# Attention and two feed-forward layers on one core: seven plain chunks and one Strassen unit of 1024 tokens in place of six and two of 768, weight sums on VectorE, later attention steps, more buffers

## The chip, the core and the metric

The kernel runs on one core of one Trainium2 chip. The metric is the device time of one execution in microseconds (us). Times of a kernel are medians over several executions; the profile is one further execution, taken with the hardware profiler. TensorE (PE) multiplies, VectorE (DVE), ScalarE (ACT) and GpSimd (POOL) work elementwise, and SyncE (SP) issues almost all DMAs from one queue. Each engine takes its own instructions in the order in which the program lists them.

## The reference

Three layers follow each other: linear attention with an RMS norm over 8 batches of 576 tokens (4608 tokens of 512 features), a bilinear feed-forward layer without a nonlinearity behind it, and a feed-forward layer with SiLU.

```python
kv = np.einsum('bhsd,bhse->bhde', k, v)
out = np.einsum('bhsd,bhde->bhse', q, kv)
rms = np.sqrt(np.mean(out * out, axis=-1, keepdims=True) + 1e-06)
x = out / rms * g_norm            # then transposed to (4608, 512)
a = x @ w1; b = x @ w2            # 512 -> 1024 each
x2 = ((a * b) @ w3) @ w_out       # 1024 -> 1024 -> 512; the kernel multiplies w3 @ w_out first
h = x2 @ w_in                     # 512 -> 2048
result = (h * (1.0 / (1.0 + np.exp(-h)))) @ w_out2   # 2048 -> 512
```

## The kernel before, in words

Every big product is made of three matmuls: both operands are split into a high part (rounded to fp32r by ScalarE) and a low part (the rest, by VectorE), and high x high, high x low and low x high are added in PSUM (`passes`, lines 111 to 115, and `run`, line 786). A split is therefore one ScalarE cast and one VectorE subtraction.

The tokens are cut into 9 chunks of 512. The program has three stretches.

**Start.** w3 @ w_out is formed (tiles `wps`, then `wch`, `wcl`), and the attention of chunk 0 is done.

**Plain phase.** The chunks in `PLAIN` (six of nine) go through the bilinear layer directly. A chunk has 8 steps; a step j has 12 matmuls into `pa` (x @ w1), 12 into `pb` (x @ w2), the product `asb` = pa * pb (ScalarE copies pa, VectorE multiplies, line 738), its split into `ch` and `cl`, and 12 matmuls of the step before into four banks `x2ps` (line 555, `g2_mm`). All these matmuls stream 512 columns. After the last step of a chunk ScalarE and VectorE copy two `x2ps` banks each into `x2o` tiles, and SP stores these to DRAM as `x2d` (lines 562 to 574).
Between the groups of 12 matmuls, other work is put by a table of events (lines 583 to 616): `event(gap, ...)` with three gaps to a step. The attention of chunk c starts at its own gap: `kv_load` and `kv_mm` (k, v and their product), `q_load`, `att_a` (matmuls `o`), `att_b` (squares `sq` and copies `ob`, ScalarE), `att_c` (matmuls `s`, the sums of squares), `att_d` (three ScalarE operations), `att_e` (two VectorE operations on `u`, then its split into `rh` and `rl`), `att_r` (matmuls `rb`, which spread `rh` and `rl` over the features), `att_x` (VectorE multiplies `ob` by `rb`) and `att_f` (the split into `xh`, `xl` for a plain chunk; a store to DRAM as `xd` for a chunk in `LATER`). Two PSUM banks, `att`, serve all these matmuls.
Also in this phase the weights of the later products are prepared, piece by piece. `ensure(done - 1)` calls `advance` (line 293) once: it stores what is ready (`flush`), loads piece n+3 (`raw`), casts piece n-1 (`bh`, line 275), decodes piece n+1 on ScalarE (lines 169, 170) and piece n on VectorE (lines 201, 203), and subtracts for piece n-1 (line 280). Three pieces make a block of weights; for every second piece of a triple, 28 times in all, `block_sums` (lines 236 to 249) forms the four sums that Strassen's scheme needs, on GpSimd, of 256 columns each, into `s12` and `s34`. `advance` is called two or three times in a step. Results go to DRAM as `wbd`.

**Strassen phase.** `UNITS` lists units of work; a unit of width w covers 2w tokens and does products of 2 x 2 blocks with 7 instead of 8 block products (Winograd's form). Units "A" do the bilinear layer for the chunks in `LATER` (6 blocks of 7 runs of 12 matmuls, each of w columns), units "B" the SiLU layer for all tokens (8 such blocks). The loop at line 919 runs over the blocks; the last block of a unit follows the first block of the next one. All matmuls are at line 799 (tiles `ps`); operands are split at lines 701 and 702, and the operand sums are on GpSimd (line 689).

## Time and profile before

| | us |
|---|---|
| median of 3 executions (1500.31 to 1504.01) | 1500.82 |
| the profiled execution | 1503.21 |
| its span, first to last instruction | 1501.1 |
| of it the start, until the first `pa` | 87.3 |
| plain phase, until the first `ps` | 530.1 |
| units A and the first B block among them | 198.2 |
| the rest of the B units | 685 |

PE is busy for 95% of the span by its records, DVE for 61%, ACT for 45%, POOL for 29%; the DMA engines moved 229 GB/s on average. A busy time of PE is not PE at its peak, since matmuls overlap in the records: how far apart they start says more. "Granted clock" (PEclk) is the share of the full TensorE clock, 1.0 for 2.4 GHz and 0.5 for 1.2 GHz. In a view of waits, "X <- Y" means that X was idle and that Y ended the wait.

### The profile page before, as it was taken

Reading aid. Unit: us, or ns where it says so; the run is one execution under the profiler, and the core shown is the slowest. Engines: PE = TensorE matmul, PEld = TensorE weight load, DVE = VectorE, ACT = ScalarE, POOL = GpSimd, SP = SyncE. Lnnn points to the kernel's source line nnn. Section 1 sums busy time; section 2 is a strip of 40 time slices with the busy share of each in tenths; the row PEclk is TensorE's granted clock in tenths of the full one; section 3 lists DMA queues with packets and bytes.
Section 4 is the critical chain, followed back from the end, with each engine's and each line's share of the span. In section 5 each row is a group of like instructions: output and inputs, shape, how many; then the busy total and the mean of one; then the engine's idle time right before and its main releaser. Section 6 shows DMA issues by size and latency. Waiting matters only on the chain.

```text
span 1501.1 us, 20241 instructions
## 1 busy us (share of the span) xinstructions
PE 1420.7 (95%) x7328; PEld 1193.1 (79%) x7328; DVE 918.0 (61%) x1208; ACT 677.6 (45%) x1099; POOL 428.8 (29%) x269
## 2 busy tenths in 40 slices
PE   7889898998897989999999999999999999999998
PEld 4567675676676657999998878787878888999998
DVE  7757555464545543448476568756785667468558
ACT  7765534344443632325153434453544443545443
POOL 0000122122221211034343354335353425245222
PEclk9999999999898999999999999999999999999999
DMA  9654467768676845488977766776668667987876
GB/s 327 206 168 163 160 229 245 262 208 274 197 243 195 270 165 183 138 297 256 348 239 252 237 186 195 229 261 191 190 206 272 190 195 245 314 246 247 291 246 206
DMA packets 160258, 344.22 MB, mean 229 GB/s; under 512 B 15264, under 2 KB 79776, under 8 KB 160160
## 3 DMA queue, kind: packets, MB, share of 16 engines
q1 hardware_dynamic: 159584, 341.90, 70.5%
q8 instruction: 58, 0.95, 0.3%
q10 hardware_dynamic: 576, 1.05, 0.2%
q14 instruction: 40, 0.33, 0.1%
HBM read 269.48 MB, written 73.40 MB: 228 GB/s over the span
## 4 chain that ended last, share of the span: by engine, by line
PE 76%; DMA 9%; DVE 6%; ACT 3%; issue 2%; SPq 2%; POOL 2%; POOLq 0%; DVEq 0%; ACTq 0%
PE ps L799 57%; DMA wbd<-s 3%; PE pb L113 2%; PE pb L115 2%; PE pb L114 2%; PE x2ps L113 2%; DMA raw<-wb_l 1%; PE pa L113 1%; PE x2ps L114 1%; PE x2ps L115 1%; PE pa L114 1%; PE pa L115 1%; DMA raw<-w3t_l 1%; PE rb L419 1%; DMA v<-v_l 1%
## 5 line engine op out<-in xcount | busy, mean ns | idle before, releaser
L799 PE MATMUL ps<-xo,w 128*128 128x384 f32 (+1 forms) x2352 | 466.8, 358 | 0.2
L799 PEld LDWEIGHTS ps<-xo,w 128*128 128x128 f32 x2352 | 422.2, 188 | 41.4 <-ACT u L831 1.7
L799 PE MATMUL ps<-go,w 128*128 128x384 f32 (+1 forms) x2016 | 414.1, 364 | 6.4 <-issue 6.4
L799 PEld LDWEIGHTS ps<-go,w 128*128 128x128 f32 x2016 | 364.3, 189 | 52.7 <-issue 12.9
L702 DVE TENSOR_TENSOR go<-g,go 128x768 fp32r<-128x768 f32 (+1 forms) x120 | 163.3, 1365 | 120.7 <-ACT go L701 120.2
L809 DVE TENSOR_TENSOR c<-ps,c 128x512 f32<-128x512 f32 (+1 forms) x280 | 162.2, 616 | 27.2 <-PE ps L799 26.2
L689 POOL TENSOR_TENSOR g_t<-g 128x768 f32<-128x768 f32 (+1 forms) x48 | 119.1, 2482 | 131.0 <-DVE g L881 65.6
L689 POOL TENSOR_TENSOR g<-g,g_t 128x768 f32<-128x768 f32 (+1 forms) x24 | 50.9, 2123 | 355.4 <-DVE go L702 355.4
L245 POOL TENSOR_TENSOR s<-t 128x256 f32<-128x256 f32 x28 | 23.2, 829 | 421.9 <-DMA wbd<-s 210.7
L701 ACT CAST go<-g 128x768 fp32r<-128x768 f32 (+1 forms) x120 | 110.9, 945 | 48.1 <-PE ps L799 40.1
L702 DVE TENSOR_TENSOR go<-g_t,go 128x768 fp32r<-128x768 f32 (+1 forms) x48 | 96.5, 2010 | 21.0 <-ACT go L701 21.0
L831 ACT COPY s<-ps 128x512 f32<-128x512 f32 (+1 forms) x40 | 21.7, 543 | 154.7 <-PE ps L799 154.7
L738 DVE TENSOR_TENSOR asb<-pb,asb 128x512 f32<-128x512 f32 x48 | 33.0, 688 | 92.6 <-PE pb L115 79.7
L113 PE MATMUL pb<-xh,w2h 128*128 128x512 f32 x192 | 83.3, 434 | 0.9 <-DVE asb L738 0.5
L113 PE MATMUL x2ps<-ch,wch 128*128 128x512 f32 x192 | 78.0, 406 | 5.6 <-ACT x2o L573 3.4
L115 PE MATMUL pb<-xh,w2l 128*128 128x512 f32 x192 | 78.8, 410 | 1.4 <-DVE w2l L230 1.4
L114 PE MATMUL pb<-xl,w2h 128*128 128x512 f32 x192 | 79.1, 412 | 0.0
L113 PE MATMUL pa<-xh,w1h 128*128 128x512 f32 x192 | 76.3, 398 | 0.0
L114 PE MATMUL pa<-xl,w1h 128*128 128x512 f32 x192 | 75.8, 395 | 0.0
L115 PE MATMUL pa<-xh,w1l 128*128 128x512 f32 x192 | 75.5, 393 | 0.0
L114 PE MATMUL x2ps<-cl,wch 128*128 128x512 f32 x192 | 75.5, 393 | 0.0
L115 PE MATMUL x2ps<-ch,wcl 128*128 128x512 f32 x192 | 75.3, 392 | 0.0
(113 smaller groups left out, 1919.5 us busy)
## 6 DMA issues: line engine op xcount, KB each, us to landing
w<-wbd SPq DMA_DIRECT2D x364, 512.0 KB, 4.4
wbd<-bh SPq DMA_DIRECT2D x72, 256.0 KB, 3.7
raw<-wb_l SPq DMA_DIRECT2D x32, 512.0 KB, 5.4
wbd<-s SPq DMA_DIRECT2D x56, 256.0 KB, 3.7
q<-q_l SPq DMA_DIRECT2D x36, 256.0 KB, 3.9
raw<-w3t_l SPq DMA_DIRECT2D x16, 512.0 KB, 6.0
k<-k_l SPq DMA_DIRECT2D x32, 256.0 KB, 4.2
v<-v_l SPq DMA_DIRECT2D x32, 256.0 KB, 4.5
```

The lines of the kernel that those rows point to most:

```text
L113: nc.tensor.matmul(out=ps_out, lhsT=ah, rhs=bh, start=first, stop=False)
L114: nc.tensor.matmul(out=ps_out, lhsT=ah, rhs=bl, start=False, stop=False)
L115: nc.tensor.matmul(out=ps_out, lhsT=al, rhs=bh, start=False, stop=last)
L245: nc.gpsimd.tensor_tensor(out=s1, in0=a21, in1=a22, op=ALU.add)
L419: nc.tensor.matmul(out=o, lhsT=spread[rows, :], rhs=half_[rows, :], start=n == 0, stop=n == 1, skip_group_check=True)
L689: nc.gpsimd.tensor_tensor(out=x, in0=x if a == place else self.src[a], in1=x if b == place else self.src[b], op=ALU.subtract)
L701: nc.scalar.copy(out=t[:, 0, :, :self.w], in_=x)
L702: self.cuts[n].tensor_tensor(out=t[:, 1, :, :self.w], in0=x, in1=t[:, 0, :, :self.w].bitcast(F32), op=ALU.subtract)
L738: nc.vector.tensor_mul(out=asb, in0=pb, in1=asb)
L799: mm = lambda a, bb, start, stop: nc.tensor.matmul(out=o, lhsT=a, rhs=bb, start=start, stop=stop, skip_group_check=True)
L809: eng.tensor_tensor(out=out_, in0=a, in1=b, op=ALU.add)
L831: nc.scalar.copy(out=t[nm, d], in_=o)
```

## The change

- `PLAIN` gets a seventh chunk, so `LATER` has two chunks (4 and 8) and one unit A of width 512 (1024 tokens) does them; before, two units A of width 384 did three chunks. The B units stay.
- `block_sums` runs on VectorE; `s12` gets two buffers, and the `bh` tiles (tag `wh`) four in place of three.
- `q` and `x2o` tiles have four buffers in place of two; all four `q_load` of a chunk are issued together, 9 gaps before that chunk's attention begins (2 before that of chunk 8).
- The attention of a chunk takes 20 gaps in place of 18, and `att_r`, `att_x` and `att_f` come two gaps later behind `att_e` (17 and 18 in place of 15 and 16).
- `advance` is called twice in a step, not two or three times; there are 8 more steps.
- `dynamic_dma_scratch_size=1024` frees SBUF, from which the buffers come.

```diff
-PLAIN = (0, 1, 2, 4, 5, 6)
+PLAIN = (0, 1, 2, 3, 5, 6, 7)
-UNITS = (("A", 384), ("A", 384), ("B", 512), ("B", 512), ("B", 512), ("B", 384), ("B", 384))
+UNITS = (("A", 512), ("B", 512), ("B", 512), ("B", 512), ("B", 384), ("B", 384))
...
-        s12 = cv.tile([P, N], F32, tag="s12", bufs=1, name=f"s12_{n}")
+        s12 = cv.tile([P, N], F32, tag="s12", bufs=2, name=f"s12_{n}")
...
-        nc.gpsimd.tensor_tensor(out=s1, in0=a21, in1=a22, op=ALU.add)
+        nc.vector.tensor_tensor(out=s1, in0=a21, in1=a22, op=ALU.add)
...
-            h = cv.tile([P, N], F32R, tag="wh", bufs=3, name=f"bh{n}_{op}")
+            h = cv.tile([P, N], F32R, tag="wh", bufs=4, name=f"bh{n}_{op}")
...
-        t = at.tile([P, N], F32, tag="q", bufs=2, name=f"q{c}_{p}")
+        t = at.tile([P, N], F32, tag="q", bufs=4, name=f"q{c}_{p}")
...
-                    o = at.tile([P, N], F32, tag="x2o", bufs=2, name=f"x2o{c}_{m}")
+                    o = at.tile([P, N], F32, tag="x2o", bufs=4, name=f"x2o{c}_{m}")
...
-            for p in range(2):
-                event(max(gap, gap_was + 11), q_load, c, p)
+            for p in range(KD):
+                event(gap_was + 11, q_load, c, p)
...
-            event(gap + 15 + i, att_r, c, i)
-            event(gap + 15 + i, att_x, c, i)
-            event(gap + 15.5 + i + 1.5 * (c in LATER), att_f, c, i)
+            event(gap + 17 + i, att_r, c, i)
+            event(gap + 17 + i, att_x, c, i)
+            event(gap + 17.5 + i + 1.5 * (c in LATER), att_f, c, i)
...
-        gap += 18 if c + 1 < B else 11
+        gap += 20 if c + 1 < B else 13
...
-                for _ in range(2 - j % 2):
-                    ensure(done - 1)
+                ensure(done - 1)
...
-    nc = bacc.Bacc("TRN2", target_bir_lowering=False, num_devices=1)
+    nc = bacc.Bacc("TRN2", target_bir_lowering=False, num_devices=1, dynamic_dma_scratch_size=1024)
```

The other three sums change engine like the first; two of the four `q_load` were in the loop over `att_a` at gap + 7 before.

What this moves is seen in the order of the instructions. On PE, at the attention of chunk 2, which falls into the first steps of chunk 1: before, the first `rb` matmuls stand between `pa` and `pb` of step 1, and since the matmuls `s` there are three groups of 12 (`pb` of step 0, `x2ps`, `pa` of step 1).

```order
L115 MATMUL pa1_1_1754<-xh1_1229,w1l1_163 128x512
L419 MATMUL rb2_0_1767<-rh2_1750,spread_113 128x512
L419 MATMUL rb2_1_1768<-rh2_1750,spread_113 128x512
L419 MATMUL rb2_0_1767<-rl2_1751,spread_113 128x512
L419 MATMUL rb2_1_1768<-rl2_1751,spread_113 128x512
L113 MATMUL pb1_1_1792<-xh1_1229,w2h1_164 128x512
```

Now they stand behind `pb` of step 2, and five groups of 12 lie between `s` and `rb` (`pa` and `pb` of step 1, `x2ps`, `pa` and `pb` of step 2).

```order
L115 MATMUL pb1_2_1850<-xh1_1291,w2l2_931 128x512
L419 MATMUL rb2_0_1866<-rh2_1788,spread_112 128x512
L419 MATMUL rb2_1_1867<-rh2_1788,spread_112 128x512
L419 MATMUL rb2_0_1866<-rl2_1789,spread_112 128x512
L419 MATMUL rb2_1_1867<-rl2_1789,spread_112 128x512
L113 MATMUL x2ps1_0_1803<-ch1_1_1783,wch1_133 128x512
```

At all other chunks, too, three groups became five. On DVE, at the same place, from the multiplication `asb` of step 0 to the low part `rl` and its use: before, the last `x2o` copies stand straight ahead of the two operations on `u`.

```order
L738 TENSOR_TENSOR asb1_0_1676<-pb1_0_1678,asb1_0_1676 128x512
L109 TENSOR_TENSOR cl1_0_1692<-asb1_0_1676,ch1_0_1691 128x512
L181 TENSOR_TENSOR t44_1707<-w1h0_158,w1l0_159 128x512
L280 TENSOR_TENSOR s34_41_1586<-s34_41_1586,bh43_5_1705 128x512
L571 COPY x2o0_1_1739<-x2ps0_1_1102 128x512
L571 COPY x2o0_3_1745<-x2ps0_3_1104 128x512
L405 SCALAR_TENSOR_TENSOR u2_1695<-s2_1660,u2_1695 128x512
L406 SCALAR_TENSOR_TENSOR u2_1695<-u2_1695,r2_1694 128x512
L109 TENSOR_TENSOR rl2_1751<-u2_1695,rh2_1750 128x512
L426 TENSOR_TENSOR ob2_0_1536<-rb2_0_1767,ob2_0_1536 128x512
```

Now `asb` of step 1 stands between the copies (line 571) and `u`, and `rl` is followed by the low part `cl` of step 1, with the use of `rb` further down.

```order
L280 TENSOR_TENSOR s34_41_1585<-s34_41_1585,bh43_5_1702 128x512
L571 COPY x2o0_1_1730<-x2ps0_1_1101 128x512
L571 COPY x2o0_3_1736<-x2ps0_3_1103 128x512
L735 TENSOR_TENSOR asb1_1_1768<-pb1_1_1770,asb1_1_1768 128x512
L405 SCALAR_TENSOR_TENSOR u2_1758<-s2_1739,u2_1758 128x512
L406 SCALAR_TENSOR_TENSOR u2_1758<-u2_1758,r2_1757 128x512
L109 TENSOR_TENSOR rl2_1789<-u2_1758,rh2_1788 128x512
L109 TENSOR_TENSOR cl1_1_1784<-asb1_1_1768,ch1_1_1783 128x512
```

The sums of a block of weights were on POOL (here those of pieces 46 and 47):

```order
L245 TENSOR_TENSOR s12_47_1830<-t46_1720 128x256
L246 TENSOR_TENSOR s12_47_1830<-s12_47_1830,t47_1777 128x256
L247 TENSOR_TENSOR s34_47_1831<-t47_1777,t46_1720 128x256
L248 TENSOR_TENSOR s34_47_1831<-t47_1777,s12_47_1830 128x256
```

On DVE they now stand between the decoding of the second piece and the subtractions for the piece before, ahead of the next `asb`:

```order
L201 SCALAR_TENSOR_TENSOR z47_1797<-raw47_1700,z47_1797 128x512
L203 SCALAR_TENSOR_TENSOR t47_1796<-t47_1796,z47_1797 128x512
L245 TENSOR_TENSOR s12_47_1840<-t46_1764 128x256
L246 TENSOR_TENSOR s12_47_1840<-s12_47_1840,t47_1796 128x256
L247 TENSOR_TENSOR s34_47_1841<-t47_1796,t46_1764 128x256
L248 TENSOR_TENSOR s34_47_1841<-t47_1796,s12_47_1840 128x256
L280 TENSOR_TENSOR t46_1764<-t46_1764,bh46_0_1834 128x256
L280 TENSOR_TENSOR s34_44_1709<-s34_44_1709,bh46_5_1836 128x512
L735 TENSOR_TENSOR asb1_2_1848<-pb1_2_1850,asb1_2_1848 128x512
```

## Rows read from the trace of the kernel before

**Rows 1.** The page: busy time of PE, and granted clock in 40 slices.
```profile
PE 1420.7 (95%) x7328; PEld 1193.1 (79%) x7328; DVE 918.0 (61%) x1208; ACT 677.6 (45%) x1099; POOL 428.8 (29%) x269
...
PEclk9999999999898999999999999999999999999999
```

**Rows 2.** Windows, all engines: length, busy of PE, PEld, DVE, ACT, POOL; PEclk, DMA.
```profile
87.30:617.40 530.10, 480.48 (x2578) 361.08 (x2577) 272.17 (x426) 233.66 (x423) 103.81 (x116) 0.95 0.63 206
617.40:815.60 198.20, 196.19 (x1093) 191.88 (x1092) 120.41 (x168) 77.75 (x131) 68.29 (x31) 0.99 0.83 269
815.60:1240.90 425.30, 422.43 (x1849) 345.83 (x1849) 283.00 (x285) 189.70 (x252) 163.28 (x60) 1.00 0.70 218
576.50:617.30 40.80, 40.80 (x181) 33.81 (x181) 13.38 (x16) 9.55 (x14) 7.37 (x4) 1.00 0.44 154
```

**Rows 3.** Timeline of PE, Strassen phase: start, length, operation, count; 384 columns, then 512.
```profile
617.37 58.43 PE L799 MATMUL ps<-xo,w 128*128 128x384 f32 x336
675.64 14.72 PE L799 MATMUL ps<-go,w 128*128 128x384 f32 x84
...
893.03 19.20 PE L799 MATMUL ps<-xo,w 128*128 128x512 f32 x84
912.07 19.20 PE L799 MATMUL ps<-go,w 128*128 128x512 f32 x84
```

**Rows 4.** Waits of PE in the plain phase: who for whom, total us, times, longest.
```profile
PE rb L419 <- ACT rh L108: 32.7, 7, 7.8
PE kvps L338 <- DMA v<-v_l: 4.7, 3, 2.7
PE x2ps L113 <- ACT x2o L573: 3.4, 1, 3.4
PE o L370 <- DMA q<-q_l: 3.2, 2, 2.2
PE x2ps L113 <- DVE x2o L571: 2.2, 1, 2.2
PE pb L115 <- DVE w2l L230: 1.4, 1, 1.4
PE rb L419 <- DVE rl L109: 1.0, 3, 0.7
```

**Rows 5.** Windows from the first `s` to the last `rb`, chunks 2 to 7.
```profile
167.72:189.05 21.33, 15.78 (x66) 10.88 (x65) 11.14 (x17) 9.85 (x17) 3.69 (x4) 0.84 0.66 219
235.64:257.17 21.53, 15.88 (x65) 10.97 (x65) 11.75 (x18) 7.75 (x14) 6.55 (x8) 0.84 0.64 202
307.66:322.42 14.76, 14.03 (x66) 9.74 (x65) 10.78 (x17) 9.50 (x17) 3.57 (x4) 1.00 0.77 252
373.01:395.90 22.89, 16.92 (x66) 11.58 (x65) 12.51 (x22) 8.96 (x16) 7.19 (x9) 0.78 0.67 209
444.45:468.44 23.99, 16.18 (x65) 11.16 (x64) 11.89 (x23) 9.85 (x17) 2.88 (x4) 0.79 0.65 204
517.15:539.96 22.81, 16.32 (x66) 11.31 (x65) 13.86 (x21) 11.80 (x22) 3.89 (x5) 0.85 0.63 216
```

**Rows 6.** Timeline of DVE ahead of `rl` of chunk 2.
```profile
175.59 0.68 DVE L571 COPY x2o<-x2ps 128x512 f32<-128x512 f32 x1
180.01 0.69 DVE L571 COPY x2o<-x2ps 128x512 f32<-128x512 f32 x1 [3.75 <-DMA x2d<-x2o]
```

**Rows 7.** Timeline of DVE ahead of `rl` of chunk 3.
```profile
245.52 1.22 DVE L280 TENSOR_TENSOR s<-s,bh 128x512 fp32r<-128x512 f32 x1
248.03 0.69 DVE L280 TENSOR_TENSOR t<-t,bh 128x512 fp32r<-128x512 f32 x1 [1.30 <-POOL s L248]
```

**Rows 8.** Groups by line in the plain phase, POOL: count, busy, mean ns, idle before.
```profile
L245 POOL TENSOR_TENSOR s<-t 128x256 f32<-128x256 f32 x28 | 23.2, 829 | 421.9 <-DMA wbd<-s 210.7 <-DVE t L203 172.2 <-DVE asb L738 39.0
```

**Rows 9.** The same for DVE: subtractions of line 280.
```profile
L280 DVE TENSOR_TENSOR s<-s,bh 128x512 fp32r<-128x512 f32 x56 | 46.4, 831 | 24.5 <-POOL s L248 12.2 <-ACT bh L275 10.9 <-DMA k<-k_l 1.3
...
L280 DVE TENSOR_TENSOR t<-t,bh 128x256 fp32r<-128x256 f32 x16 | 6.8, 423 | 37.2 <-POOL s L245 37.2
```

More of the change, by code (lines that the diff above doesn't have):

```diff
@@ L241, in block_sums @@
         a21, a22, a11, a12 = t0[:, :2 * P], t0[:, 2 * P:], t1[:, :2 * P], t1[:, 2 * P:]
-        s12 = cv.tile([P, N], F32, tag="s12", bufs=1, name=f"s12_{n}")
+        s12 = cv.tile([P, N], F32, tag="s12", bufs=2, name=f"s12_{n}")
         s34 = cv.tile([P, N], F32, tag="s34", bufs=2, name=f"s34_{n}")
         s1, s2, s3, s4 = s12[:, :2 * P], s12[:, 2 * P:], s34[:, :2 * P], s34[:, 2 * P:]
-        nc.gpsimd.tensor_tensor(out=s1, in0=a21, in1=a22, op=ALU.add)
-        nc.gpsimd.tensor_tensor(out=s2, in0=s1, in1=a11, op=ALU.subtract)
-        nc.gpsimd.tensor_tensor(out=s3, in0=a11, in1=a21, op=ALU.subtract)
-        nc.gpsimd.tensor_tensor(out=s4, in0=a12, in1=s2, op=ALU.subtract)
+        nc.vector.tensor_tensor(out=s1, in0=a21, in1=a22, op=ALU.add)
+        nc.vector.tensor_tensor(out=s2, in0=s1, in1=a11, op=ALU.subtract)
+        nc.vector.tensor_tensor(out=s3, in0=a11, in1=a21, op=ALU.subtract)
+        nc.vector.tensor_tensor(out=s4, in0=a12, in1=s2, op=ALU.subtract)
         sums[n] = s12, s34
@@ L599, in fused @@
         if c > 1:
-            for p in range(2):
-                event(max(gap, gap_was + 11), q_load, c, p)
+            for p in range(KD):
+                event(gap_was + 11, q_load, c, p)
         for i in range(2):
@@ L604, in fused @@
             event(gap + 7 + 3 * i, att_b, c, i)
-            if i == 0:
-                for p in (2, 3):
-                    event(gap + 7, q_load, c, p)
         event(gap + 12, att_c, c)
```

## The prediction

> **What bounds the kernel now.** I began with the page's busy times and clock row, went on to windows by stage, then to the waits of PE inside the worst stage. PE is busy for 95% of the span, and no other engine comes near it [rows 1]; so the time is PE's work, at the spacing at which it issues matmuls, plus its stalls. By stage the stalls are not spread evenly: in the plain phase PE's records cover 480.5 of 530.1 us and the mean granted clock is 0.95, while the B units run at 422.4 of 425.3 us and full clock [rows 2].
>
> The spacing is read from starts. At 384 columns 336 matmuls take 675.64 - 617.37 = 58.27 us, 173.4 ns each; at 512 columns 84 take 912.07 - 893.03 = 19.04 us, 226.7 ns each [rows 3]. The undisturbed end of the plain phase gives the same: 181 matmuls touch a window of 40.8 us, so 180 spacings of 226.7 ns [rows 2]. A 384-column matmul thus costs 0.452 ns a column and a 512-column one 0.443.
>
> In the plain phase one wait dominates: `rb` for `rh`, 32.7 us, and 1.0 us for `rl` [rows 4]. The windows from `s` to the second `rb` show what it costs in all [rows 5]. They hold the same matmuls at every chunk. Chunk 4 needed 14.76 us with 0.73 us idle (14.76 - 14.03) at full clock, so 14.03 us is the undisturbed length; the others needed 21.3 to 24.0 us, with a granted clock of 0.78 to 0.85: PE stands still for 5.6 to 7.8 us, and a stretch at half clock, 1.2 GHz, follows. The cause is upstream. The chain `s`, `r`, `u`, `rh` goes through the queues of ACT and DVE behind other work. At chunk 2 (and 6, where the end of a chunk coincides too) DVE holds an `x2o` copy for 3.75 us until a store frees one of two buffers, with `u` behind it [rows 6]. At chunk 3 (5 and 7 have the same order) the decoding of weight pieces stands ahead of `u`, with a subtraction that waits 1.30 us for POOL's sums and another stretched to 1.22 us beside them [rows 7].
>
> **The change, part by part.**
>
> *Units against chunk.* The two A units and the B block among them take 198.2 us [rows 2]. Afterwards that stretch is 6 + 1 blocks of 512. The 425.3 us behind it hold 22 such blocks with their small stalls, 19.33 us each [rows 2]; 7 x 19.33 = 135.3 us, a gain of 62.9 (64.9 if all run at 19.04 us). The seventh chunk adds 8 steps of 36 matmuls, 288 x 226.7 ns = 65.3 us; its attention was done in the plain phase before too and adds nothing. Net **+2.4 us**; +0.4 at best, +5 if the change of widths stalls as it does now (198.2 - 12 x 14.57 - 19.04 = 4.3 us over clean blocks, in place of 2.0). So this part alone is no gain: the number of columns rises, and only the dearer 384-column form that goes pays for it.
>
> Beside this sum stands a rule that speaks against the trade. The rows give 11 ns over the columns' own time at both widths (512 / 2.4 = 213.3 ns, 384 / 2.4 = 160 ns; the spacing is 226.7 and 173.4) [rows 3]. The Trainium skill, "TensorE: Matmul & The Clock Gate", section "Back-to-back issue gap", puts an isolated matmul at N / 2.4 + 2.5 ns, that is 215.8 and 162.5. By that, 792 matmuls of 512 for 1008 of 384 would cost 7.1 us more, by the rows' spacing 4.7; the forecast would be 2.4 us later. The trace disagrees with the page on the fixed part, and the row is used.
>
> *The attention's later place, and the buffers of `x2o`.* Five groups of 12 now lie between `s` and `rb`, at 12 x 226.7 ns = 2.72 us each, so with the 1 us of `s` itself there are about 14.6 us before PE asks for `rh`; before, three groups gave 9.2. The undisturbed chain of chunk 4 needed about 9.9 us (9.2 + 0.73). The others needed 9.2 plus their idle time, 14.7 to 17.0 us [rows 5]. Even an unshortened chain would leave waits of 0.1 to 2.4 us in place of 5.6 to 7.8; and it is shortened, since four `x2o` buffers take the 3.75 us away at chunks 2 and 6 [rows 6], and in the new order DVE has nothing between `asb` and `u` at chunks 2 and 5, two to four operations at most others and ten short ones at chunk 6, where it had five to eight at the five bad chunks. The excess over 14.03 us in the six windows is 7.30 + 7.50 + 0.73 + 8.86 + 9.96 + 8.78 = 43.1 us [rows 5]. Their idle time is 32.2 us of the 33.7 us of the two waits [rows 4]; the remaining 1.5 belongs to chunks 1 and 8. Together 44.6 us, of which I take **-44** (-33 if some 2 us stay at each of five chunks). What is late next is `asb`: its multiplication now stands ahead of `u` at chunks 2 and 5, and PE needs it only two groups later.
>
> *Other waits.* `x2ps` for the copies (3.4 + 2.2) and `o` for `q` (3.2) [rows 4] have four buffers now, and the loads of `q` go out 16 gaps, more than five steps, ahead of `att_a`; SP no longer holds later loads behind a `q` or `x2o` that waits. `kvps` for `v` (4.7) and `pb` for `w2l` (1.4) keep their distances. Behind these waits, too, the clock fell: 0.05 of 530 us missing at half speed is 53 us at 1.2 GHz, of which the five windows hold 0.16 x 2 x 21.3 and so on, 41 us [rows 2, 5]. The other 12 us cost up to 6, some 40% on top of the 14.9 us of waits. For `x2o` and `q` that is 8.8 x 1.4 = 12.3 us; of the rest (8.5) I take 2.5, since SP is less held up. **-14.8** (-9 to -21).
>
> *Sums on DVE.* 28 x 4 operations of 256 columns. The nearest row on DVE, a subtraction of 256 columns, is 423 ns [rows 9]: 112 x 0.42 = 47 us. DVE is busy for 272 of 530 us there [rows 2]; with 47 us, and some 1.4 us for each of 8 more steps, that is about 330 of 540. PE needs `asb` only after two further groups, 5.4 us, which covers one set of sums (1.7 us). Against that DVE loses 37.2 + 12.2 us of waits for POOL [rows 9] and the stretching beside POOL (a mean of 831 ns over 56 operations against the 0.69 us of an undisturbed one, 8 us) [rows 7, 9]. On PE's path the price lies between below zero (less DVE waiting) and 28 x 1.7 = 47 us if nothing covered it. I take **+2**, near the covered end, because DVE has 40% to spare and two advances a step are fewer than before.
>
> *The rest.* The fourth `bh` buffer and the two of `s12` are what the sums on DVE need; counted there. The scratch size moves only addresses; 0.
>
> Sum: 2.4 - 44 - 14.8 + 2 = **-54.4 us**. The profiled execution took 1503.2 us (span 1501.1) and becomes 1448.8; the median of the runs shown lies 2.4 us lower, so 1500.8 - 54.4 = **1446.4 us**.
>
> **The rivals.**
> 1. *The stall moves instead of going.* The chain's length came from queues, and with more on DVE it may grow with the distance: at chunks where four sums stand ahead of `u` (chunk 6) or where `asb` does (2 and 5), 2 us of waiting and a stretch at 1.2 GHz would stay at each of five chunks, and the loads of `v` and `w2l` stay as late as now. For it: chains of 14.7 to 17.0 us against 14.6. Against it: the causes that rows 6 and 7 show are both removed. -33 for the attention, -12 for the rest, +5 for the sums: 1463 us.
> 2. *DVE takes over POOL's waits, and the kernel is slower than before.* POOL waited 210.7 us, 23 times, for the store of `s12`/`s34` (`wbd`) [rows 8], 9.2 us each, which cost nothing while only POOL stood still. On DVE such a wait holds the next `asb`, and with it `pb`. With two buffers for each the store was issued two to three advances earlier, a step or more, so it should have landed. It decides from a loss on PE of 56 / 28 = 2.0 us for each set of sums; at 3 us, with half clock behind, 28 x 3 = 84 us: 1444 + 84 = 1528 us.
> 3. *All stalls go*, also those for `v` and `w2l`, and the sums cost nothing: 2.4 - 44.6 - 21 = -63, 1438 us.
>
> **How the numbers follow.** Forecast (1440 to 1456) 0.60, rival 1 (1456 to 1480) 0.22, rival 3 (below 1440) 0.11, rival 2 and any time above the median 0.05; within 0.3% of the median, which is about what a measurement of this kernel can tell from no change, 0.02. The range runs from rival 3's 1436 (64.9 for the units) to 1470, past rival 1's own time, and leaves out about 2 in 10. Faster 0.93, same 0.02, slower 0.05.
>
> **What would show it.** In the profile of the changed kernel: the plain phase about 540 us long, 65 us more for the chunk and 55 less for stalls; the stretch of the A unit and the first B block about 135 us; windows from `s` to the second `rb` without idle time; no waits of PE for `x2o` or `q`; clock near 1.0 in the plain phase; DVE at 60% there with hardly a wait ahead of line 245. Wrong would be: PE waiting for `asb` in many steps (rival 2), `rb` still waiting for `rh` (rival 1), or blocks of the A unit above 20 us, DVE then being too slow for splits of 1024 columns.

## The result, and the profile after

The changed kernel takes 1436.98 us (median of 4 executions, 1431.62 to 1439.04); beside it, on the same chip, the kernel before took 1501.4. The ratio is 0.9563, 95% interval 0.9534 to 0.9592: 64.4 us less. The forecast was 1446.4; by the ratio the time is 1500.8 x 0.9563 = 1435.2, 0.8 us under the low end of the range (1436 to 1470). It is close to the 1438 us of the third rival, "All stalls go", which had a chance of 0.11. One execution of a kernel below, the one with the early place, ran slow, at 4919 us, and is left out of its median.

The page of the changed kernel, which answers to [rows 1]: busy times (us, share of the span, instructions) and the granted clock in 40 slices.

```profile
PE 1396.9 (98%) x7112; PEld 1150.0 (80%) x7112; DVE 916.2 (64%) x1263; ACT 665.1 (47%) x1064; POOL 311.6 (22%) x143
...
PEclk9999999999999999999999999999999999999999
```

PE is busy for 98% in place of 95%, and no slice shows a lowered clock. By stage (length, busy of PE, PEld, DVE, ACT, POOL; PEclk, DMA share, GB/s), to be read beside [rows 2]: the start, the plain phase, the A unit with the first B block, the rest.

```profile
0.00:83.64 83.64, 62.87 (x385) 43.41 (x385) 63.83 (x100) 63.61 (x111) 2.12 (x21) 1.00 0.76 261
83.64:609.71 526.07, 522.79 (x2865) 402.38 (x2864) 311.70 (x560) 245.87 (x445) 9.60 (x4) 1.00 0.63 209
609.71:744.09 134.38, 133.83 (x589) 110.24 (x588) 79.03 (x89) 52.78 (x74) 45.14 (x17) 1.00 0.68 213
744.09:1429.40 685.31, 677.37 (x3277) 593.96 (x3275) 461.62 (x515) 302.83 (x436) 254.77 (x101) 1.00 0.73 233
```

The plain phase holds a seventh chunk, 65.3 us of matmuls, and is still 4.0 us shorter (530.1 - 526.1): 69.3 us of stalls went. The A unit with its B block takes 134.4 us in place of 198.2, 63.8 less. The rest, 685.3 us, is as before. The start is 3.6 us shorter, with no change in it but two more loads of `q`: its granted clock is 1.00 here and was 0.96 in the profile of before, and in the profiles of the experiments, whose starts do the same work but for these loads, it lies between 0.89 and 1.00, with starts of 91.4 to 85.2 us. Sum: 65.3 - 69.3 - 63.8 - 3.6 = -71.4, which is the difference of the two spans, 71.6. This profiled execution (1431.6 us) is the fastest of the four, and part of that is the start; so kernels are compared below by medians and by the length of the plain phase.

All that is left of [rows 4] in the plain phase (waits of PE: for whom, total us, times, longest):

```profile
PE kvps L338 <- DMA v<-v_l: 1.6, 2, 1.0
PE pb L115 <- DVE w2l L230: 1.4, 1, 1.4
PE pb L113 <- ACT w2h L217: 0.3, 1, 0.3
```

The 33.7 us for `rb` and the 8.8 us for `x2o` and `q` are gone. The windows from `s` to the last `rb` at chunks 2 and 6, answering to [rows 5], hold two more groups of 12, as the new order has it:

```profile
168.20:187.39 19.19, 19.19 (x90) 14.18 (x89) 15.07 (x29) 10.27 (x19) 0.00 (x0) 1.00 0.57 203
...
423.58:442.76 19.18, 19.18 (x90) 14.17 (x89) 13.02 (x26) 10.14 (x18) 0.00 (x0) 1.00 0.53 178
```

They have no idle time: 19.19 - 2 x 2.72 = 13.75 us, against 14.03 at the undisturbed chunk 4 before and 21.3 to 24.0 elsewhere. On DVE (plain phase, by line and shape: count, busy us, mean ns, idle before), beside [rows 8, 9]:

```profile
L735 DVE TENSOR_TENSOR asb<-pb,asb 128x512 f32<-128x512 f32 x56 | 38.7, 690 | 124.5 <-PE pb L115 118.3 <-ACT asb L730 6.2
L280 DVE TENSOR_TENSOR s<-s,bh 128x512 fp32r<-128x512 f32 x56 | 38.3, 686 | 21.6 <-ACT bh L275 21.4
...
L245 DVE TENSOR_TENSOR s<-t 128x256 f32<-128x256 f32 x28 | 11.7, 419 | 0.0
```

The sums wait for nothing, and the subtractions of line 280 are no longer stretched: 686 ns in place of 831.

### The profile page after: what moved, and what is told of

It reads as the page before. It is cut to its first block, busy times and chain, and to the rows that moved or that the text cites. A ratio compares the mean times of both kernels' runs of the same rounds, so it can differ in the third digit from the quotient of the medians.

```text
span 1429.5 us, 19284 instructions
## 1 busy us (share of the span) xinstructions
PE 1396.9 (98%) x7112; PEld 1150.0 (80%) x7112; DVE 916.2 (64%) x1263; ACT 665.1 (47%) x1064; POOL 311.6 (22%) x143
## 4 chain that ended last, share of the span: by engine, by line
PE 93%; DVE 2%; DMA 2%; issue 1%; ACT 1%; SPq 0%; DVEq 0%; ACTq 0%
PE ps L795 56%; PE pb L113 4%; PE x2ps L113 4%; PE pa L113 4%; PE pb L115 4%; PE pb L114 3%; PE x2ps L115 3%; PE pa L115 3%; PE x2ps L114 3%; PE pa L114 3%; DMA raw<-w3t_l 1%; PE kvps L338 1%; PE o L370 1%; PE rb L419 1%; DVE z L201 1%
## 5 line engine op out<-in xcount | busy, mean ns | idle before, releaser
L795 PE MATMUL ps<-xo,w 128*128 128x512 f32 (+1 forms) x2016 | 425.4, 371 | 0.1
L795 PEld LDWEIGHTS ps<-xo,w 128*128 128x128 f32 x2016 | 368.8, 188 | 53.7 <-ACT u L827 1.3
L795 PE MATMUL ps<-go,w 128*128 128x512 f32 (+1 forms) x1848 | 392.4, 370 | 5.1 <-issue 5.1
L699 DVE TENSOR_TENSOR go<-g,go 128x1024 fp32r<-128x1024 f32 (+1 forms) x110 | 156.2, 1424 | 112.9 <-ACT go L698 112.5
L686 POOL TENSOR_TENSOR x_t<-x2r 128x1024 f32<-128x1024 f32 (+1 forms) x12 | 30.3, 2522 | 564.4 <-DMA w<-wbd 563.9
L686 POOL TENSOR_TENSOR g_t<-g 128x1024 f32<-128x1024 f32 (+1 forms) x44 | 113.0, 2569 | 108.6 <-ACT g L838 62.5
L698 ACT CAST go<-g 128x1024 fp32r<-128x1024 f32 (+1 forms) x110 | 105.0, 974 | 46.2 <-PE ps L795 35.0
L686 POOL TENSOR_TENSOR g<-g,g_t 128x1024 f32<-128x1024 f32 (+1 forms) x22 | 48.4, 2200 | 342.8 <-DVE go L699 342.8
L699 DVE TENSOR_TENSOR go<-g_t,go 128x1024 fp32r<-128x1024 f32 (+1 forms) x44 | 93.6, 2127 | 20.7 <-ACT go L698 20.7
L108 ACT CAST ch<-asb 128x512 fp32r<-128x512 f32 x56 | 35.0, 626 | 123.1 <-DVE asb L735 123.1
```

The costliest lines, as they stand in the source:

```text
L108: nc.scalar.copy(out=h, in_=x)
L686: nc.gpsimd.tensor_tensor(out=x, in0=x if a == place else self.src[a], in1=x if b == place else self.src[b], op=ALU.subtract)
L698: nc.scalar.copy(out=t[:, 0, :, :self.w], in_=x)
L699: self.cuts[n].tensor_tensor(out=t[:, 1, :, :self.w], in0=x, in1=t[:, 0, :, :self.w].bitcast(F32), op=ALU.subtract)
L795: mm = lambda a, bb, start, stop: nc.tensor.matmul(out=o, lhsT=a, rhs=bb, start=start, stop=stop, skip_group_check=True)
```

## The experiments

The ratios are to the kernel before on the same chip, with 95% intervals; they tell kernels apart from about 0.4% (6 us) on, and the plain phase, from one profile each, is given for what is smaller. The "late place" is `att_r` and what follows it at +17, the "early" one at +15; "3/2" and "2" are the advances in a step.

| kernel | median us | ratio | plain phase us |
|---|---|---|---|
| before | 1500.8 | 1 | 530.1 (6 chunks) |
| changed | 1437.0 | 0.9563 (0.9534 to 0.9592) | 526.1 (7 chunks) |
| **before, with one part or some:** | | | |
| late place | 1503.3 | 0.9998 (0.9985 to 1.0012) | 529.3 (6) |
| four `x2o` buffers | 1481.8 | 0.9859 (0.9837 to 0.9881) | 504.8 (6) |
| all but units, gaps, advances, `q` | 1476.4 | 0.9829 (0.9812 to 0.9846) | 501.5 (6) |
| units (seven chunks, one A unit) | 1505.4 | 1.0020 (1.0003 to 1.0037) | 592.1 |
| units, 20 gaps | 1481.7 | 0.9848 (0.9816 to 0.9880) | 570.3 |
| units, 2 advances | 1485.5 | 0.9875 (0.9838 to 0.9912) | 579.7 |
| units, 20 gaps, 2 advances, `x2o` | 1444.1 | 0.9610 (0.9583 to 0.9637) | 534.3 |
| the same and two `s12` buffers | 1441.3 | 0.9585 (0.9565 to 0.9606) | 530.7 |
| **changed, with something undone:** | | | |
| sums on POOL | 1435.5 | 0.9535 (0.9496 to 0.9574) | 526.3 |
| one `s12` buffer | 1440.0 | 0.9568 (0.9526 to 0.9610) | 528.7 |
| `q` loads and tiles as before | 1437.1 | 0.9559 (0.9522 to 0.9597) | 527.2 |
| two `x2o` buffers | 1448.7 | 0.9612 (0.9568 to 0.9655) | 540.7 |
| early place | 1439.2 (3 executions) | 0.9561 (0.9517 to 0.9605) | 530.8 |
| 3/2 advances | 1444.2 | 0.9598 (0.9574 to 0.9623) | 535.9 |
| 18 gaps, late place | 1442.3 | 0.9589 (0.9558 to 0.9620) | 531.4 |
| 18 gaps, early place | 1459.8 | 0.9699 (0.9669 to 0.9729) | 551.9 |

**First question: is it the attention's later place and the buffers of `x2o`, as the prediction has it?** The theory was put to the test by adding its parts to the kernel before, and by taking them from the changed one.

*The late place alone, in the kernel before.*

```diff
-            event(gap + 15 + i, att_r, c, i)
-            event(gap + 15 + i, att_x, c, i)
+            event(gap + (17 if c < 8 else 15) + i, att_r, c, i)
+            event(gap + (17 if c < 8 else 15) + i, att_x, c, i)
```

> The kernel before with att_r, att_x and att_f two gaps later at chunks 1 to 7 and nothing else. Theory: the two further groups add 5.4 us of cover, so waits for rh of 0 to 1.5 us stay where 5.6 to 7.8 us were; the stalls for x2o (9.5 us) and q (6 us) stay: 40 us less, 1458 to 1468 us. Rival (the chain lengthens with what now stands ahead of it, so the stall moves): half of the rh waits stay, 1475 to 1490 us.

Measured: 1503.3 us, no gain that can be told (at most 2.3 us by the interval). What was expected to go did go, and came back elsewhere. PE's largest waits behind the first attention:

```profile
PE rb L419 <- DVE ob L426: 10.3, 6, 3.3
...
PE kvps L338 <- DVE ob L426: 5.9, 6, 1.8
PE rb L419 <- ACT rh L108: 4.5, 4, 2.0
```

The wait for `rh` fell from 32.7 to 4.5 us, but the second pair of `rb` now waits for `ob`, the multiplications by `rb` that free the two `att` banks, and so does the next chunk's `kvps`, whose first gap (18 gaps on) is now also that of the second pair. Why DVE is late with `ob` is seen in its timeline at chunk 2 (start, length, operation, count, idle time before): from 186.1 us on it has one advance after the other ahead of `ob`.

```profile
188.65 0.68 DVE L738 TENSOR_TENSOR asb<-pb,asb 128x512 f32<-128x512 f32 x1
...
190.63 0.68 DVE L201 SCALAR_TENSOR_TENSOR z<-raw,z 128x512 uint32<-128x512 uint32 x1
191.34 1.10 DVE L203 SCALAR_TENSOR_TENSOR t<-t,z 128x512 uint32<-128x512 uint32 x1
...
192.71 1.21 DVE L280 TENSOR_TENSOR s<-s,bh 128x512 fp32r<-128x512 f32 x1
193.84 1.28 DVE L426 TENSOR_TENSOR ob<-rb,ob 128x512 f32<-128x512 f32 x2
```

So the part on which the prediction put most of its gain is worth nothing by itself. The title of its first rival, "The stall moves instead of going", fits what happens there, but not its mechanism: that rival expects waits for `rh` to stay, and the wait for `ob` stands neither there nor in the sum.

*The late place taken from the changed kernel* (+17 back to +15, the 20 gaps stay).

> The changed kernel with att_r, att_x and att_f two gaps earlier, as before (the 20 gaps for a chunk's attention stay): three groups of 12 matmuls between s and rb in place of five. Theory (both the distance and what stands in the queues count): the chain is short now, as at chunk 4 of the kernel before, 9.9 us against 9.2 us of cover, so 0.7 us of waiting at most chunks and up to 3 at some, clock mostly full: PE waits for rh 5 to 12 us in all, median 1443 to 1455 us. Rival 1 (the distance is all): the waits of 33 us with the half clock come back, median 1475 to 1485 us. Rival 2 (the distance is nothing, the emptier queues did it): 1436 to 1439 us.

Measured: 0.9561 against 0.9563, and 1439.2 us, at the upper end of rival 2's 1436 to 1439 and below the theory's 1443. The waits for `rh` and `rl` come to 2.1 us, none over 0.8, and the plain phase is 4.7 us longer. With the other edits in place, the late place is hardly needed.

*Four `x2o` buffers alone, in the kernel before; two in the changed kernel.*

```diff
-                    o = at.tile([P, N], F32, tag="x2o", bufs=2, name=f"x2o{c}_{m}")
+                    o = at.tile([P, N], F32, tag="x2o", bufs=4, name=f"x2o{c}_{m}")
...
-    nc = bacc.Bacc("TRN2", target_bir_lowering=False, num_devices=1)
+    nc = bacc.Bacc("TRN2", target_bir_lowering=False, num_devices=1, dynamic_dma_scratch_size=1024)
```

The second line makes room for the buffers and goes with them in every run that adds them to the kernel before; no run has it alone. The changed kernel with two buffers keeps it.

> The kernel before with four x2o buffers (and the small DMA scratch that makes room) and nothing else. Theory: the waits of x2ps go (5.6 us, 9.5 us with the slow clock behind them), and u of chunks 2 and 6 comes 3.75 us earlier, which takes about half of their rh waits (7 us with the clock): 1484 to 1494 us. Rival (the rh waits are set elsewhere): 1491 to 1496 us with rh waits as long as before at every chunk.

> The changed kernel with two x2o buffers in place of four. Theory: at each of the six chunk ends the third and fourth copy wait for a store (3.75 us on DVE and about as long on ACT), so PE waits for x2ps at several chunk ends as it did in the kernel before (about 9.5 us with the slow clock behind it for five ends, so 11 us for six), and u of chunk 2 comes late again: 1445 to 1455 us. Rival (the stores are quicker now, because SP no longer holds them behind q loads): x2ps waits stay under 2 us in all and the median is 1436 to 1440 us.

Measured: 21 us less in the kernel before, a little more than expected, and 7 to 12 us more in the changed one (by the ratios 0.0049 x 1500.8 = 7.4; by the medians 11.8). In the kernel before the waits for `x2ps` are gone, and of those for `rh` this is left:

```profile
PE rb L419 <- ACT rh L108: 23.2, 6, 6.8
```

The second was right in size, not in its way: `x2ps` waits for the copies only 1.8 us. DVE stands still for 21.3 us, six times, ahead of its `x2o` copies; the copies come later, so their four stores go out over 5.1 us in place of 2.8 at the end of the third chunk, and behind these on SP's queue wait the loads of `v`. PE's waits, and then the window around the longest:

```profile
PE kvps L338 <- DMA v<-v_l: 3.4, 2, 2.5
...
PE x2ps L113 <- DVE x2o L571: 1.4, 1, 1.4
```

```profile
335.00:352.00 17.00, 13.57 (x75) 10.77 (x74) 7.54 (x14) 3.81 (x8) 0.00 (x0) 0.80 0.96 322
```

A wait of 2.5 us, one of 0.9 behind it, and a granted clock of 0.80 in these 17 us. Around a wait of 1.6 us for `ob` (185 to 200 us) it is 0.89, and around the waits for `x2ps` (418 to 432 us) 0.88.

*Sums on DVE.* Three runs: the sums back on POOL; one `s12` buffer with the sums on DVE; the loads of `q` as before (the first two of a chunk 7 gaps ahead of its `att_a`, not 9 as its text has it), since POOL's and DVE's tiles are freed by stores in the same queue.

```diff
-        nc.vector.tensor_tensor(out=s1, in0=a21, in1=a22, op=ALU.add)
+        nc.gpsimd.tensor_tensor(out=s1, in0=a21, in1=a22, op=ALU.add)
```

> The changed kernel with one part undone: the four sums of a block of weights are formed on POOL again (two buffers for s12 and s34 stay). Theory (the stalls went because of the later place of the attention and the four x2o buffers; the sums' engine is a side matter): DVE waits 1 to 1.5 us for POOL at some 28 places, about 35 us in all, but the two extra groups before the rb matmuls (5.4 us) and before asb's use cover them, so PE loses 0 to 8 us and the median is 1437 to 1445 us. Rival (the wait for POOL's sums in DVE's queue was what made the chain to rh long at chunks 3, 5 and 7): PE waits for rh again at three or more chunks, 1.3 to 2.5 us each with half clock behind it, median 1450 us or more.

> The changed kernel with one buffer for s12 in place of two, the sums still on DVE. This is the slower rival of the prediction made on purpose: DVE has to wait for the store of the last s12. Theory: POOL waited 9.2 us for it 23 times in the kernel before; on DVE the same wait holds the next asb, of which two groups (5.4 us) cover a part, so PE loses 2 to 4 us with half clock behind it at 20 or more sets of sums: 1490 to 1560 us. Rival (with the quicker queue the store has landed by then, or DVE runs far enough ahead): under 10 us more, 1437 to 1447 us.

> The changed kernel with the loads of q as before: two q tiles in place of four, two loads 9 gaps ahead at most and two at att_a itself. Theory: the waits of o for q come back (6 us with the slow clock behind them, in the kernel before), and loads that SP queues behind a q that waits for its buffer come later: 1441 to 1447 us, with waits of PE for q or v. Rival (with 20 gaps the loads have time enough): 1435 to 1439 us, no wait for q over 0.5 us.

Measured: 0.9535, 0.9568 and 0.9559: each the changed kernel's time. None of the three matters by itself; the slower rival, for which the run with one buffer expected 1490 to 1560 us, does not appear: the sums on DVE wait for no store that PE would notice (asb: 1.5 us in two waits).

**Second question: what, then?** The kernel before with all these edits, but with its own units, 18 gaps and 3/2 advances:

> The kernel before with its own units (six plain chunks, two A units of 768 tokens) but with the edits against the stalls: sums on DVE with two s12 buffers, four bh buffers, four x2o buffers, att_r and what follows it two gaps later at chunks 1 to 7, small DMA scratch. The loads of q and the advances stay as before. Theory: the units give nothing and these edits give nearly all: rb waits gone (44 us), x2o waits gone (9), some 6 us for q left: 1440 to 1455 us. Rival (the thinner weight preparation of the seventh chunk is needed, as DVE is too full with three advances in a step): rb or asb waits remain, 1465 us or more.

Measured: 1476.4 us, on the rival's side, and only some 5 us less than with the `x2o` buffers alone, which the two intervals do not tell apart. PE waits for `ob` again:

```profile
PE rb L419 <- DVE ob L426: 12.5, 6, 3.0
PE kvps L338 <- DVE ob L426: 6.0, 6, 1.3
```

So more than half of the gain is in what was left out. The units alone:

```diff
-PLAIN = (0, 1, 2, 4, 5, 6)
+PLAIN = (0, 1, 2, 3, 5, 6, 7)
-UNITS = (("A", 384), ("A", 384), ("B", 512), ...
+UNITS = (("A", 512), ("B", 512), ...
```

> The kernel before with one part of the change alone: seven plain chunks and one A unit of 1024 tokens (sums on POOL, old buffers, attention at 18 gaps, advances in turns of three and two). Theory (this part is 2.4 us dearer by itself, and the stalls in the plain phase stay or grow with one more chunk end): the stretch of the A unit and the first B block falls by about 63 us, the plain phase grows by 65 us and by up to 8 us of stalls: 1500 to 1512 us. Rival (the trade of units was itself most of the gain, since a further chunk thins the weight preparation out over more steps and so empties the queues): the stalls of the plain phase fall by 20 us or more, 1485 us or less.

Measured: 1505.4 us, ratio 1.0020: 3.0 us dearer, as the theory had it; the waits for `rh` remain:

```profile
PE rb L419 <- ACT rh L108: 34.1, 6, 10.3
```

What is left to test are the 20 gaps and the advances. This is where the new theory came from: 18 gaps are six steps, so that with 18 the attention of chunks 1 to 7 meets the steps in the same phase, and 20 gaps change the phase from chunk to chunk. Two runs:

```diff
-        gap += 18 if c + 1 < B else 11
+        gap += 20 if c + 1 < B else 13
```

> The kernel before with seven plain chunks and one A unit, and with 20 gaps for a chunk's attention in place of 18 (13 for the last but one); att_r and the rest of it stay at +15, the buffers, the q loads, POOL's sums and the advances as before. New theory, formed since taking the later att_r back cost nothing: it is the phase. With 18 gaps, six steps exactly, s always falls between pa and pb of a step, and u stands in DVE's queue behind the asb of that same step and four to eight operations after it, so the chain from s to rh takes 12 to 17 us at five chunks. With 20 gaps the phase differs from chunk to chunk and u stands right behind an asb at chunks 2 and 5, and at 3, 6 and 8 behind one that is over before s. So against the same kernel with 18 gaps (1505 us): waits for rh of 34 us fall to 10 us or less, and 25 to 40 us of time go: 1465 to 1480 us. Rival (the three advances in every second step, or POOL's sums, or the q loads made the chain long): waits for rh of 20 us or more stay, 1488 us or more.

> The changed kernel with the attention's own places as before: 18 gaps for a chunk (11 for the last but one) and att_r and the rest at +15; sums on DVE, buffers, q loads and two advances in a step stay as changed. Theory (the phase of 18 gaps makes the chain long): u stands behind the asb of its own step and 7 to 12 operations at chunks 2 to 7, four of them sums of 0.42 us: chains of 10 to 12 us against 8.3 us of cover, so waits for rh of 1.5 to 4 us at six chunks, 12 to 20 us in all with half clock behind: 1452 to 1470 us. Rival (the advances or the q loads were the cause, the phase is nothing): waits for rh under 5 us, 1436 to 1443 us.

Measured: 1481.7 us, 24 us less than with the units alone (just short of the 25 to 40 expected); and 1459.8 us, 23 us above the changed kernel and inside the 1452 to 1470 expected. The waits for `rh`, first with the units and 20 gaps, then in the changed kernel with 18 gaps and the early place:

```profile
PE rb L419 <- ACT rh L108: 9.7, 4, 4.4
```

```profile
PE rb L419 <- ACT rh L108: 12.2, 7, 2.8
```

The timelines of DVE at chunk 3 show the phase. With 18 gaps and the early place, the end of `s` lies at 232.30 us; `asb` of the same step comes only at 235.35, since PE does `pb` of that step behind `s`, and `u` (line 405) has seven operations between itself and `asb`:

```profile
235.35 0.69 DVE L735 TENSOR_TENSOR asb<-pb,asb 128x512 f32<-128x512 f32 x1 [4.58 <-PE pb L115]
236.73 0.69 DVE L109 TENSOR_TENSOR cl<-asb,ch 128x512 fp32r<-128x512 f32 x1 [0.69 <-ACT ch L108]
237.34 0.68 DVE L181 TENSOR_TENSOR t<-w1h,w1l 128x512 f32<-128x512 f32 x1
237.94 0.42 DVE L245 TENSOR_TENSOR s<-t 128x256 f32<-128x256 f32 x1
...
239.07 0.42 DVE L248 TENSOR_TENSOR s<-t,s 128x256 f32<-128x256 f32 x1
239.41 0.68 DVE L280 TENSOR_TENSOR s<-s,bh 128x512 fp32r<-128x512 f32 x1
240.01 0.69 DVE L405 SCALAR_TENSOR_TENSOR u<-s,u 128x512 f32<-128x512 f32 x1
```

That is 7.7 us from the end of `s` to `u`. With 20 gaps and the early place, `s` ends at 237.27 us, behind `pb` of its step: `asb` is over by then.

```profile
236.38 0.69 DVE L735 TENSOR_TENSOR asb<-pb,asb 128x512 f32<-128x512 f32 x1 [4.66 <-PE pb L115]
237.76 0.69 DVE L109 TENSOR_TENSOR cl<-asb,ch 128x512 fp32r<-128x512 f32 x1 [0.69 <-ACT ch L108]
...
239.70 0.68 DVE L280 TENSOR_TENSOR s<-s,bh 128x512 fp32r<-128x512 f32 x1
241.32 0.69 DVE L405 SCALAR_TENSOR_TENSOR u<-s,u 128x512 f32<-128x512 f32 x1 [0.94 <-ACT u L399]
```

Here only four operations lie between `asb` and `u`, and `u` starts 4.05 us after `s`; what it waits for last (0.94 us) is no longer DVE's own queue but ScalarE's part of `u`. Over chunks 2 to 7 the first `rh` is ready 13.9, 14.0, 8.3, 14.3, 16.2 and 14.8 us after `s` in the kernel before, 11.0, 9.8, 9.8, 9.8, 11.2 and 10.0 us with 18 gaps and two advances, and 8.5, 6.1, 7.7, 8.5, 6.0 and 9.1 with 20 gaps (early place), where PE asks for it 8.3 us after `s`.

*Two advances, in the kernel before with the units.*

```diff
-                for _ in range(2 - j % 2):
-                    ensure(done - 1)
+                ensure(done - 1)
```

> The kernel before with seven plain chunks and one A unit, and with two advances in every step in place of three and two in turn; attention at 18 gaps, buffers, q loads and POOL's sums as before. Theory (phase first, the advances second): at chunks 3, 5 and 7 the first advance of the step puts fewer casts ahead of r and the decoding and subtractions ahead of u become fewer, so those chains (12 to 13 us after s) shorten by 2 to 4 us; chunks 2 and 6, where x2o copies stand ahead, stay: waits for rh of 18 to 26 us where the same kernel with three and two has 34, 1488 to 1498 us. Rival (three advances in a step were the cause): under 12 us of rh waits, 1480 us or less.

Measured: 1485.5 us, 20 us less than with the units alone, between the theory (1488 to 1498) and its rival (1480 or less). The waits for `rh` fell from 34.1 to 13.6 us, further than expected, but a new one came: PE for `asb`, behind DVE, behind POOL's sums, behind the store of the single `s12`. The rows of the three engines (waits behind the first attention, then DVE and POOL):

```profile
PE pb L113 <- DVE asb L738: 16.3, 6, 3.6
PE rb L419 <- ACT rh L108: 13.6, 6, 5.0
```

```profile
DVE t L280 <- POOL s L245: 70.6, 11, 11.8
```

```profile
POOL s L245 <- DMA wbd<-s: 287.7, 21, 28.0
```

The single buffer alone does not bring this: the units with three and two advances have it too, and PE waits for no product `asb` there. With 20 gaps and four `x2o` buffers in addition 2.3 us of the wait are left (below); which of these two takes it away is not shown.

**Third question: is this the whole of it?** Units, 20 gaps, two advances and four `x2o` buffers in the kernel before, and then a second `s12` buffer in addition:

> The kernel before with four of the changes only: seven plain chunks and one A unit of 1024 tokens, 20 gaps for a chunk's attention, two advances in a step, four x2o buffers (with the small DMA scratch that makes room). Left as before: sums on POOL with one s12 buffer, three bh buffers, two q tiles with their late loads, att_r at +15. Theory (these four carry the whole gain; what is left as before cost nothing singly): 1437 to 1447 us, waits for rh 5 us or less. Rival (a single s12 buffer on POOL stalls DVE, and with it PE at asb, as it did with two advances at 18 gaps, 16 us of waits): 1452 us or more, waits of PE for asb of 8 us or more.

> As the run of four changes, with two buffers for s12 in addition; the sums are on POOL still. Theory: 1436 to 1442 us, no wait for asb over 1 us, so the second s12 buffer does what little is left, and the sums' change of engine is worth nothing. Rival (the sums have to leave POOL for that): no better than the run of four changes, by more than 5 us over the whole changed kernel.

Measured: 1444.1 and 1441.3 us. By the ratios on 1500.8 us the four carry 58.5 of 65.6 us, and 62.3 with the second `s12` buffer; the latter's interval (0.9565 to 0.9606) and that of the whole change (0.9534 to 0.9592) overlap, so the last 3 us are not told apart. The sums are on POOL in both. With one buffer, little of the wait for `asb` is left:

```profile
PE pb L113 <- DVE asb L738: 2.3, 2, 2.0
```

Added up one by one, the four give 1.0020 - 1 = +0.2%, 0.9848 - 1.0020 = -1.7%, 0.9875 - 1.0020 = -1.5% and 0.9859 - 1 = -1.4%: -4.4%, against -3.9% together. That is the same within the intervals: they overlap little, if at all, when they are added to the kernel before.

**Fourth question: why can they be undone so cheaply in the changed kernel?**

> The changed kernel with three and two advances in turn in place of two in every step. Theory: the phase of 20 gaps and the later att_r leave 13.8 us for a chain that gets at most 2 to 4 us longer (from 6 to 10 us), so no rh waits return; the steps with three advances hold ACT and DVE 2.5 us longer, with waits of PE for asb at some of them: 1437 to 1448 us. Rival (two advances are needed, whatever the attention's place): 1450 us or more.

> The changed kernel with 18 gaps (11 for the last but one) for a chunk's attention and att_r and the rest at +17 as changed; all else as changed. Against the same kernel with att_r at +15 (1460 us) this shows what the later place does by itself where the phase is bad. Theory: the waits for rh (12 us) go, but the second rb pair now stands at the gap in which the next chunk's kv_mm starts, and both need the two att banks that DVE's multiplications ob free: waits for ob of 8 to 16 us in their place, 1450 to 1465 us. Rival (the later place covers the chain and the banks come free in time): 1440 us or less.

Measured: 1444.2 us with 3/2 advances, 1442.3 us with 18 gaps and the late place. No wait for `rh` is left in either, as both theories on the place had it; with 3/2 advances the expected waits for `asb` don't come either, but one of 6.5 us for a load of `v` does. What PE waits for in them behind the first attention:

With 3/2 advances:

```profile
PE kvps L338 <- DMA v<-v_l: 6.7, 2, 6.5
PE rb L419 <- DVE ob L426: 1.3, 1, 1.3
```

With 18 gaps and the late place:

```profile
PE kvps L338 <- DVE ob L426: 5.7, 6, 1.3
...
PE o L370 <- DVE ob L426: 0.8, 1, 0.8
```

The suspicion about the banks was right in kind (`kvps` waits for `ob` six times, up to 1.3 us) but not in size: 6.5 us in place of 8 to 16, without a fall of the clock; DVE has less ahead of `ob` than in the run of the late place alone (at chunk 2 five operations between `rl` and `ob` in place of nine). The time, 1442.3 us, lies 2 us above what the rival expected and 8 below the theory. The plain phases with two advances and all buffers form a square:

| | early place | late place |
|---|---|---|
| 18 gaps | 551.9 | 531.4 |
| 20 gaps | 530.8 | 526.1 |

Either the phase or the distance is enough, 21.1 and 20.5 us; the second of them adds 4.7 or 5.3. With 3/2 advances the late place and 20 gaps give 535.9; the late place at 18 gaps 501.5 us with six chunks, that is 566.8 with 65.3 for a seventh. So at 18 gaps the late place brings 20.5 us with two advances, and with 3/2 advances, together with the sums on DVE and their buffers, no more than 3.3 (504.8 to 501.5). A reading that fits is that it pays only where DVE has room between the steps, and that the two advances give that room: PE's waits for `ob` are 18.9 us in the one run and 6.5 in the other. No run changes the advances alone there, so this is not shown.

## Why the prediction was right and wrong

- **The bound** (PE's work and its stalls in the plain phase): right. 69.3 us of stalls went there, and no other engine took their place.
- **Units against chunk, +2.4:** right. The A unit with its B block gained 63.8 us (forecast 62.9), the units alone cost 3.0 us (0.5 to 5.6 by the interval). The formula for an isolated matmul in the Trainium skill, "TensorE: Matmul & The Clock Gate", section "Back-to-back issue gap", would have made that some 4.8, by an estimate: the interval holds both, so the time doesn't decide between them. The spacing does: in the changed kernel the first of 84 matmuls of 512 columns and the first of the next 84 are 19.04 us apart, 226.7 ns for each, not 215.8. The prediction's "11 ns over the columns' own time" is a slip: its own figures give 13.4 at both widths (226.7 - 213.3 and 173.4 - 160). Its sum does not use it.

```profile
685.87 19.20 PE L795 MATMUL ps<-go,w 128*128 128x512 f32 x84
704.91 19.20 PE L795 MATMUL ps<-xo,w 128*128 128x512 f32 x84
```

- **The attention, -44:** right in size, wrong in its cause. This is the step of the mechanism that failed: "Five groups of 12 now lie between `s` and `rb`", with chains of 14.7 to 17.0 us that the distance would cover. The distance did cover the chain in the run of the late place alone, where the waits for `rh` fell to 4.5 us, but the 16.2 us of waits for `ob` that took their place are not in the sum, and that run gained 0.0 us. In the changed kernel its removal cost 4.7 us of the plain phase. What went there was the chain itself: it fell to 6.0 to 9.1 us, through the phase of 20 gaps (24 us when added to the units), the evener advances (20 us when added to the units) and the copies' buffers. The prediction read the new order of DVE rightly, nothing between `asb` and `u` at chunks 2 and 5, but counted it with the later place; it is the same with the early one, since `u` has its place from `att_e`, which the change does not move within an attention. What moved is the attention against the steps. The 20 gaps stand in the list of changes and have no term in the sum, and neither have the advances for this wait. That -44 came out all the same is luck in part. The next wait that was feared, for `asb`, did not come.
- **`x2o`:** forecast at 5.6 x 1.4 = 7.8 us for the copies' waits, and as a part of the attention's term at chunks 2 and 6. Alone it gave 21 us in the kernel before (waits for `rh` 23.2 in place of 32.7 us, none for `x2ps`) and 7 to 12 in the changed one. Right in kind.
- **`q`:** 3.2 x 1.4 = 4.5 of the 12.3 us of that term were its wait. With its old loads the changed kernel is as fast (0.9559 against 0.9563), and PE waits for no `q` in the plain phase. It does not with the units and 20 gaps alone, or with the units and two advances, either, so the new loads are not needed; which edit takes the wait away is not shown.
- **The size:** this is the term of the sum that was mis-sized. The plain phase was forecast at 530.1 + 65.3 - 56.8 = 538.6 us and took 526.1, 12.5 less. Of the 69.3 us of stalls that went, 44.6 us are what the prediction counted for the attention; by difference, the other waits gave 24.7 us, where its sum has 14.8. These 9.9 us are most of the miss; the rest are the 2 us added for the sums and 0.6 us of the attention. Of the 9.9 us, 3.0 were waits for `v` and `w2l` that the sum kept (6.0, where 3.0 are left). The other 6.9 us are, by difference, what the short waits cost on top of their length: the prediction put 40% on them for a lowered clock, and they bring nearly as much again as they last (last section). How much of that is the clock is not shown. The range's low end came from the third rival, which used the same 40%.
- **Sums on DVE, +2:** nothing measurable, either way (0.9535 with POOL). The cover was there, as argued: DVE still waits 118 us for `pb` ahead of `asb`.
- **The slower rival:** with one `s12` buffer, DVE's sums cost PE 1.5 us. A wait of DVE behind the store of `s12` reached PE in full, 16.3 us, only in the run with the sums on POOL, one buffer, 18 gaps and two advances.

What stays open: which of the other edits (the late place, the fourth `bh` buffer, `q`, the sums on DVE) makes up the 3 to 7 us between the four or five edits and the whole change; the intervals overlap there. Also open is why the wait for `asb` with one `s12` buffer nearly goes with 20 gaps and four `x2o` buffers, and whether the smaller DMA scratch does anything by itself.

## What to carry to other kernels

Where a table of due times repeats with a period, its phase against the main loop can decide what stands ahead of a short critical chain; look at the order of the feeding engine at several repetitions, and ask for each edit by itself whether it would give that order. A stall with three causes (queue ahead of it, phase, distance) can look like any one of them: adding a part to the old kernel and taking it from the new one give different answers, and both are needed. A wait that goes away by moving the consumer can come back at whatever the consumer holds, here two PSUM banks.

## What the runs showed of the hardware

In these runs a short wait often costs PE more than its length. At chunk 3 of the run with 18 gaps and the early place, PE waits 1.44 us for `rh`, then works on at full spacing, and from about 244.5 to about 248 us matmuls of 512 columns start 0.43 us apart, at half clock (1.2 GHz):

```profile
242.13 0.56 PE L419 MATMUL rb<-rh,spread 32*128 32x512 f32 x2 [1.44 <-ACT rh L108]
...
244.08 0.40 PE L113 MATMUL pb<-xh,w2h 128*128 128x512 f32 x1
244.32 0.39 PE L114 MATMUL pb<-xl,w2h 128*128 128x512 f32 x1
...
245.34 0.63 PE L114 MATMUL pb<-xl,w2h 128*128 128x512 f32 x1
245.77 0.63 PE L115 MATMUL pb<-xh,w2l 128*128 128x512 f32 x1
```

The window of that chunk, from `s` to the second `rb`, to be read beside [rows 5]:

```profile
231.23:248.52 17.29, 15.69 (x66) 10.81 (x65) 7.45 (x14) 6.23 (x11) 0.00 (x0) 0.90 0.59 190
```

Its matmuls are busy for 15.69 us in place of 14.03, so 1.6 us of standing still (17.29 - 15.69) brought 1.7 us at the lower clock with it. Chunks 2 and 4 to 7 show the like, with granted clocks of 0.83 to 0.91: 1.6 to 3.0 us of standing still and 1.6 to 3.1 us on top. In [rows 5] 5.6 to 7.8 us of standing still brought 1.8 to 2.9 us, much the same amount, so its share is smaller the longer the wait. By difference, the other waits of [rows 4] (14.9 us) and their consequences cost some 28 us in the kernel before: the 24.7 us that went and the 3.3 that are left. Not every wait does it: those of 0.7 to 0.8 us with 20 gaps and the early place, the six of up to 1.3 us with 18 gaps and the late place, and the 1.4 us for `w2l` in the changed kernel were followed by no such stretch; the granted clock of these plain phases is 1.00.

The subtractions of line 280 take longer while the sums are on POOL: 831 ns in the kernel before, 686 in the changed one, and 858 in the changed one with the sums back on POOL, whose time is the same.
